# Up-projection of the last two superblocks by Strassen's algorithm, in a transformer block on one Trainium2 core

## The chip, the cores and the metric

One core of one Trainium2 chip runs the whole kernel. Its engines work side by side and wait for each other through semaphores: PE (TensorE, matmuls into PSUM), DVE (VectorE), ACT (ScalarE), POOL (GpSimd), and SP (SyncE), which here issues every DMA. The metric is the device time of one execution in microseconds; the kernel before takes 467.36 us, the median of three runs (466.88 to 467.95).

## The reference

One transformer block over 2048 tokens of 512 features: a modulated layer norm, linear attention with 32 heads and a learned two-sided softmax feature map, a residual; then a second modulated layer norm, and an MLP with 1376 hidden features:

```python
h = _layernorm(x) * (1 + ca) + sa
x = x + ga * A(h)                    # attention: qkv, feature maps, phi_q (phi_k^T V) / den, wo
h = _layernorm(x) * (1 + cb) + sb
y = _layernorm(h)
x = x + gb * (gelu(y @ w1 + b1) @ w2 + b2)
```

The change is in `y @ w1`, the up-projection: (2048 x 512) times (512 x 1376).

## The kernel before, in words

Every large matrix product is made in three matmuls of rounded numbers: an operand is split into a high part (rounded to the fp32r type by ACT) and a low part (what is left, by a subtraction on DVE or POOL), and `mm3` adds high x high, high x low and low x high into one PSUM bank. A matmul contracts 128 features and gives 128 x 512 numbers, so a product with 512 input features takes 4 x 3 = 12 matmuls.

Tokens come in 8 blocks of 256 (b = 0 to 7) for the attention and in 4 superblocks of 512 for the MLP. The first third projects q, k and v and adds up the key-value sums; q is kept in DRAM. Then, for each block: softmax parts and their scaling (tiles eq, ez, rcq; mostly POOL and DVE), transposition through DRAM (eb, et_dram, eT), the product with the sums (po), the output projection (pw), and the second pair of layer norms in three steps, la, lb and lc, each with statistics on DVE and a power on POOL (rsb, rsc). The result h goes through a DVE transposition (yb) to DRAM (yt_dram), comes back as yf, and `y_split` makes its high and low parts, yT.

A superblock's MLP: `up(b, fc)` makes one of 11 chunks of 128 hidden features (the last holds 96) in a bank pg, applies the GELU on ACT and splits the result into g; `down(b, fc)` multiplies g with w2 into four banks py, one for 128 tokens each, that gather over all chunks. `mlp_out` adds py to x and stores it. While superblock b's MLP runs, the attention of blocks 2b+2 and 2b+3 runs beside it; superblock 3 has nothing beside it.

The order of the work is written out by hand. `Later` and `Held` hold back every instruction under the name of its item, the engine's letter (p PE, a ACT, v DVE, g POOL, s SP) and its part of the program; `nc.issue()` then takes them in the order of the strings in `ISSUE`. Each engine runs its instructions in that order, so an instruction that waits holds up all behind it on its engine. `SLOTS` says which of 19 equal SBUF buffers and of 8 PSUM banks a tile takes. Weights of the up-projection lie in SBUF as high and low parts for the whole program (w, wlast), those of the down-projection in w2a and w2b.

Because all instructions are issued by `Later`, every row of the profile carries one line number; instructions are told apart by their tiles.

Of the kernel before, what the change touches and what calls it, by code (L numbers as in the profile page):

```python
# [47 lines left out]
    "e93cf0idhabf4g55a2h17e4i27ce25986gi96f88af4a115357h8gbbf584dec522e4g0bai8761904137ecd23b5bh77df6ae2i"  # L48
    "8507c4i322a9h829i53i9a528962i4bafe6a8h7b52ge1d00gcfggf19dgd0d2c56g9ceecc6eb0c0gc87h0g9f37i53ffb62ci7"
    "c45450fab338f8fb8c78b4374hg7h8d14263afbaab619aae55df204db9bf32fb313dd9bhe3047gagi11e",  # L50
    "bank":
    "1264710140570135353253136162435026621304533162143502472521023727652170445605353123554624602715375317"
    "153573175304761253153253215213576546037217123132712723327513246406462",
    "st6a": "01110010",
    "sta": "01010101",
    "vea": "10101001",
    "rsa": "01110110",
    "nma": "10001001",
    "dz": "001001011",
    "mxk": "1010100110011010",  # L60
    "smk": "0100011001010101",
    "rck": "0010011010101001",
    "mxq": "01011011",
    "smq": "00000000",
    "rcq": "02002110",
    "den": "10000010",
    "rd": "11010110",
    "st6b0": "10111000",
    "stb0": "01010111",
    "veb0": "01100100",  # L70
    "rsb0": "01110010",
    "st6c0": "11010100",
    "stc0": "11001000",
    "vec0": "00110010",
    "rsc0": "11011010",
    "nmc0": "11110010",
    "st6b1": "11110111",
    "stb1": "00000011",
    "veb1": "10111001",
    "rsb1": "01101110",  # L80
    "st6c1": "11100001",
    "stc1": "01000010",
    "vec1": "10100011",
    "rsc1": "01000111",
    "nmc1": "11011001",
# [3 lines left out]
-init.v -init.v -init.p db.s x0.s x1.s dk.s dq.s dm.s si.a si.v dk.s si.v bd.v si.v dk.s sr.p dq.s s0.v s0.v s0.v  # L89
s0.v s0.v s0.v s0.g sr.a dm.s s1.v s1.v s1.v n0.v s1.v n0.v dm.s s1.v s1.v n0.v s1.g fk.p dm.s ok.a x.s fq.p n0.a  # L90
ok.v fq.p oq.a n1.v n1.v m.v m.g n1.a h0.p dk.s oq.v fk.p m.v m.a n1.v ++x.s fk.p oq.a f.v ok.a oq.v fq.p n1.a ok.v
fq.p f.a m.g m.v f.v h0.p m.v pf.p n1.v m.a m.g n1.s oq.a f.v ok.a dv.s m.v m.g f.a n1.s m.a f.v pf.p n1.s m.v m.v
oq.a n1.s m.a f.v dv.s fk.p m.v ok.v f.a bg.s f.v +x.s pf.p oq.v f.v s.v f.a ok.a f.v vs.a oq.v q0.p s.v s.v s.v s.v
ok.v n1.s q1.p bg.s s.v ++s.v s.g +bg.s vs.a vs.v vs.g n.v ++s.v n.a n.v pf.p n.a n.v n.v pv1.p bg.g ++s.v k0.v n.s
h.a q0.a +s.v n.s h.a +s.v n.s q1.a +bg.g +s.v ++s.v n.s ++s.v k0.v f.a pv0.p ++++x.s h.a +bg.v f.g +bg.s h.a +s.v
+s.v k0.v f.a +bg.s +s.v ++s.v +bg.s k1.v +s.g k1.v f.g
""",
    """
pk1.p n.v -k0.v n.a n.v +s.g e.v bg.a bg.g -k0.a +bg.s +++s.v -n.s pk0.p e.v ++x.s e.g bg.a -v1.a bg.g bg.v +n.v
+n.v k1.v bg.g bg.a -k1.v q0.p +n.a -k1.v +bg.g n.a bg.v +n.a n.v +bg.g +n.v pv1.p h.a k1.v h.a e.g +n.v +bg.a n.v  # L100
++++x.s bg.a e.g ++s.v h.a n.s q1.p -k0.v e.g h.a n.s q0.a n.s f.a ++s.v +n.s f.a f.g k1.v n.s +++s.v +n.s pv0.p
q1.a k0.v f.g e.a +bg.v ++s.v -k1.a k1.v +bg.s ++s.v ++s.v -k0.v -bg.a
""",
    """
pk1.p +++s.v --k0.g --v0.a +s.v ++s.v bg.v -n.s n.s -bg.v n.s +s.g -k0.v -v1.a pv0.p --v0.v --k1.v bg.g ++s.v +n.v
--v1.v bg.v +n.a +++s.v bg.a pv1.p --bg.v bg.a +n.v bg.v -k0.v +n.a e.v -k1.a n.s h.a ++s.v --k1.v pk0.p e.g h.a
k1.v f.a ++s.v --k1.g e.v h.a +++s.v +++s.v -k0.v q1.p f.g -k1.v -k0.a h.a --v1.v k0.v -v0.a +++s.v -v0.v --v0.v
k1.v f.a k1.v -m0.p f.g -m1.p +n.v bg.p q0.p +n.v e.g bg.a q1.a k0.v +n.s +h.a +++s.v k1.v +n.s +h.a +++s.g -k1.v
+n.s e.g v1.v
""",  # L110
    """
pk1.p -k0.v -bg.s -q0.a -e.g n.s -k0.v h.a -q1.s f.a --e.v --k1.g -k0.a -bg.s ----init.v --v1.v --e.a pk0.p n.s k1.v
-bg.s f.g --v1.v --k0.v h.a -bg.s -bg.s f.a -bg.s +s.g -k0.v f.g
""",
    """
pk0.p --k0.v -k1.v -bg.s ---k0.v ---v0.v -k0.v ---k0.g n.v -k1.v pk1.p n.a -k1.v --v0.a -k0.v --k1.a --k0.g -k0.v
n.v --v0.v +n.v -k0.v n.a pv1.p --k1.v -k0.a --v1.a --k1.v +n.a k0.v --k1.g h.a k1.v --m0.p h.a --m1.p k0.v h.a
-m0.p h.a -bg.g -pv0.p n.v -k1.a --v0.v n.v f.a -k0.v n.s f.a n.s f.g -bg.a --v1.v -k0.v n.s pv0.p +n.v k1.v v1.a
n.s f.g -v1.v -v0.v +n.a k0.v k1.v -bg.g k1.v -pv1.p -k1.v n.s k0.v -bg.g +n.v k0.a +n.v
""",  # L120
    """
pk1.p -k1.a --k1.v n.s -k0.v n.s --v0.a --k0.g --v1.a n.s ----e.v h.a n.s -bg.a pk0.p ----e.s --k1.g -k1.v h.a h.a
-k0.v f.a n.s k1.v h.a -bg.g -bg.s --m1.p k0.v f.a -m0.p --v0.v -v1.v -m1.p +++lp0.s pv0.p v1.v -k1.v f.g k0.v k1.v
f.g ----e.v k1.v
""",
# [73 lines left out]
out.v d.p out.s out.v out.v out.s out.s  # L199
""",  # L200
]
W2A = 6
AHEAD = 4
NT = 1
BUFS = 19
ALIGN = 64
NE = 2


class Held:  # L210

# [958 lines left out]
```

## Time and profile before

| what | value |
|---|---|
| median of three runs | 467.36 us |
| span of the profiled execution | 466.6 us, 0.8 below the median; the page lists no other time of it |
| PE busy | 458.5 us, 98% |
| DVE busy | 317.1 us, 68% |
| POOL busy | 279.7 us, 60% |
| ACT busy | 234.6 us, 50% |
| DMA | 68.05 MB, 146 GB/s on average |

How to read the rows: in a group of instructions stand engine, operation, out<-in with tile names, shape and count, then busy us and mean ns of one, then the idle time of the engine before them and who ended it. In a chain of waits and a timeline each row starts with its start and its length in us. A stretch of the span shows, after the length, the busy us of PE, PEld (weight loads), DVE, ACT and POOL with their instruction counts, then the granted clock, the DMA share and GB/s. A matmul's own duration overlaps with its neighbours', so its price in a stream is read from the chain.

### The profile page before, as it was taken

Reading aid. Unit: us, or ns where it says so; the run is one execution under the profiler, and the core shown is the slowest. Engines: PE = TensorE matmul, PEld = TensorE weight load, DVE = VectorE, ACT = ScalarE, POOL = GpSimd, SP = SyncE. Lnnn points to the kernel's source line nnn. Section 1 sums busy time; section 2 is a strip of 40 time slices with the busy share of each in tenths; the row PEclk is TensorE's granted clock in tenths of the full one; section 3 lists DMA queues with packets and bytes.
Section 4 is the critical chain, followed back from the end, with each engine's and each line's share of the span. In section 5 each row is a group of like instructions: output and inputs, shape, how many; then the busy total and the mean of one; then the engine's idle time right before and its main releaser. Section 6 shows DMA issues by size and latency. Waiting matters only on the chain.

```text
span 466.6 us, 8536 instructions
## 1 busy us (share of the span) xinstructions
PE 458.5 (98%) x3297; PEld 372.3 (80%) x3297; DVE 317.1 (68%) x612; ACT 234.6 (50%) x381; POOL 279.7 (60%) x233
## 2 busy tenths in 40 slices
PE   8999999999999999999999999999999999999996
PEld 5887888888878878978787878787788788788884
DVE  5999999989938599389797579896484472221113
ACT  4757866767440827848537743176133234422221
POOL 2369587999799998989899684756721020300000
PEclk9999999999999999999999999999999999999999
DMA  8998738492372664836837728077445504000003
GB/s 311 382 311 301 195 84 276 95 269 55 100 257 95 189 209 90 244 104 139 224 135 160 225 53 241 1 130 178 143 90 136 122 14 93 15 30 1 1 1 135
DMA packets 83673, 68.05 MB, mean 146 GB/s; under 512 B 54688, under 2 KB 70960, under 8 KB 83376
## 3 DMA queue, kind: packets, MB, share of 16 engines
q1 hardware_dynamic: 83632, 67.50, 50.9%
q8 instruction: 26, 0.43, 0.4%
q14 instruction: 15, 0.12, 0.1%
HBM read 44.94 MB, written 22.55 MB: 145 GB/s over the span
## 4 chain that ended last, share of the span: by engine, by line
PE 85%; DMA 5%; DVE 4%; POOL 2%; issue 1%; ACT 1%; SPq 0%; DVEq 0%; POOLq 0%; ACTq 0%
PE py L218 25%; PE pg L218 24%; PE pv L218 8%; PE pk L218 8%; PE pw L218 8%; PE pq L218 7%; PE pkv L218 2%; DMA wm<-in_wmodT 2%; PE po L218 1%; DVE pw L218 1%; DMA eT<-et_dram 1%; DMA wms<-in_wmodT 1%; DMA xt<-in_x 1%; PE qp L218 1%; POOL w2a L218 1%
## 5 line engine op out<-in xcount | busy, mean ns | idle before, releaser
L218 PE MATMUL pg<-yT,w 128*128 128x512 f32 (+1 forms) x528 | 115.3, 371 | 0.6 <-DVE yT L218 0.3
L218 PEld LDWEIGHTS pg<-yT,w 128*128 128x128 f32 x528 | 92.8, 188 | 18.5 <-DVE yT L218 0.5
L218 ACT ACTIVATE pg<-pg,blob 128x512 f32<-128x512 f32 x44 | 29.1, 662 | 100.6 <-PE pg L218 100.4
L218 PE MATMUL py<-w2a,g 128*128 128x512 f32 x288 | 70.7, 391 | 0.0
L218 DVE TENSOR_TENSOR g<-pg,g 128x512 fp32r<-128x512 f32 x40 | 27.2, 680 | 61.7 <-ACT g L218 61.7
L218 PEld LDWEIGHTS py<-w2a,g 128*128 128x128 f32 x288 | 53.6, 188 | 12.6 <-issue 1.6
L218 PE MATMUL pk<-wk,hT 128*128 128x512 f32 x192 | 46.2, 392 | 0.8 <-ACT hT L218 0.7
L218 PE MATMUL py<-w2b,g 128*128 128x512 f32 x192 | 46.9, 391 | 0.0
L218 PE MATMUL pv<-wvh,hT 128*128 128x512 f32 x192 | 45.9, 392 | 0.0
L218 PE MATMUL pw<-wo,oT 128*128 128x512 f32 x192 | 45.4, 390 | 0.0
L218 PE MATMUL pq<-wq,hT 128*128 128x512 f32 x192 | 45.3, 391 | 0.0
L218 PEld LDWEIGHTS pk<-wk,hT 128*128 128x128 f32 x192 | 35.6, 188 | 9.1 <-ACT hT L218 1.1
L218 PEld LDWEIGHTS py<-w2b,g 128*128 128x128 f32 x192 | 35.9, 188 | 8.1 <-issue 0.7
L218 PEld LDWEIGHTS pw<-wo,oT 128*128 128x128 f32 x192 | 35.9, 188 | 7.8 <-issue 0.4
L218 PEld LDWEIGHTS pv<-wvh,hT 128*128 128x128 f32 x192 | 35.7, 188 | 7.5
L218 PEld LDWEIGHTS pq<-wq,hT 128*128 128x128 f32 x192 | 35.8, 188 | 7.3
L218 POOL TENSOR_TENSOR ez<-eq,zb 128x1024 f32<-128x1024 f32 x15 | 36.8, 2469 | 5.5 <-ACT last L218 3.0
L218 POOL TENSOR_TENSOR yT<-yf,yT 128x256 fp32r<-128x256 f32 x24 | 17.2, 742 | 35.1 <-ACT yT L218 35.0
L218 POOL TENSOR_TENSOR ek<-ek,rck 128x1024 f32<-128x1024 f32 x16 | 30.8, 1939 | 4.5 <-DVE rck L218 2.3
L218 POOL TENSOR_TENSOR eq<-eq,rcq 128x1024 f32<-128x1024 f32 x15 | 28.9, 1937 | 0.3
L218 ACT ACTIVATE g<-pg 128x512 fp32r<-128x512 f32 x40 | 24.0, 599 | 9.5 <-PE pg L218 4.4
L218 DVE TENSOR_REDUCE smq<-eq 128x64 f32<-128x1024 f32 x16 | 19.2, 1207 | 6.8 <-ACT eq L218 6.8
(153 smaller groups left out, 783.4 us busy)
## 6 DMA issues: line engine op xcount, KB each, us to landing
et_dram<-eb SPq DMA_DIRECT2D x48, 128.0 KB, 2.9
eT<-et_dram SPq DMA_DIRECT2D x12, 512.0 KB, 5.1
xt<-in_x SPq DMA_DIRECT2D x8, 512.0 KB, 6.1
wms<-in_wmodT SPq DMA_DIRECT2D x8, 512.0 KB, 5.9
x<-in_x SPq DMA_DIRECT2D x8, 512.0 KB, 5.2
out<-x SPq DMA_DIRECT2D x15, 256.0 KB, 2.5
nt_dram<-nb SPq DMA_DIRECT2D x28, 128.0 KB, 3.4
hd<-nt_dram SPq DMA_DIRECT2D x7, 512.0 KB, 5.5
```

The source lines that it names most:

```text
L218: return lambda *a, **k: self.later.hold(self.letter, lambda: f(*a, **k))
```

## The change

Superblocks 2 and 3 are no longer two MLPs one after the other. For each of five pairs of hidden chunks (2j, 2j+1), the pair and the two superblocks form a 2 x 2 product: two chunks of weights by two halves of the 512 input features, times two halves of the features by two superblocks. Winograd's form of Strassen's algorithm makes it from seven half products (each 2 x 3 = 6 matmuls) instead of eight:

- `even(j)`: chunk 2j of superblock 2 from two half products as usual; the first of them is also kept (tile s1) for later.
- `weight_sums(j)`: loads the pair's weights again, makes four sums of them on POOL, and puts their high and low parts over the weights that are no longer needed (and into a new tile, sum1).
- `token_sums(h)`: for each half of the tokens, four differences of the two superblocks' inputs on DVE (tiles yr and tz), and their high and low parts (t14, t23).
- `odd(j)`: the other five half products, into banks pb and pc, with additions on DVE into u tiles between them; gives chunk 2j+1 of superblock 2 and both chunks of superblock 3.

The down-projection of superblock 2 is cut in two: its even and last chunks are gathered first and added to x; the odd ones are gathered at the very end, in one bank for each 128 tokens, and added then. The inputs of superblocks 2 and 3 are read as they lie in DRAM, without the rearrangement that `y_split` made; so x of these tokens is written to DRAM (x1_dram) and read back in the same order (x1n), and the host does not rearrange the second half of the output.

All strings of `SLOTS` and `ISSUE` are new; in the first part the opening rows stand nearly as before. There are 20 equal buffers instead of 19; the small statistics tiles mostly have one buffer.

```diff
+    def half_product(o, w, t, first):
+        for k in range(2):
+            for wj, tj in ((0, 0), (0, 1), (1, 0)):
+                nc.tensor.matmul(o, w[wj][:, k], t[tj][:, k], start=first and k + wj + tj == 0, stop=k + wj == 2,
+                                 skip_group_check=True)
 ...
         if b < NY:
             return
         yT = y_half(b)
+        if b >= 4:
+            for k2 in range(2):
+                src = YF[b][:, 2 * k2:2 * k2 + 2]
+                nc.scalar.activation(yT[0][k2], src, AF.Copy)
+                nc.gpsimd.tensor_sub(yT[1][k2], src, f32(yT[0][k2]))
+            return
 ...
+    def even(j):
+        nc.item(f"u{j}")
+        p = ps_mm("pg")
+        (a11, a12), _ = pair(j)
+        half_product(p, a11, [h[0] for h in YT[2]], True)
+        if j % 2 == 0:
+            PS["s"] = wtile("s1", [2, 512])
+        S1[j] = PS["s"][:, j % 2]
+        nc.scalar.activation(S1[j], p, AF.Copy)
+        half_product(p, a12, [h[1] for h in YT[2]], False)
+        G[2, 2 * j] = gelu(p, 2 * j)
+
+    def weight_sums(j):
+        nc.item(f"s{j}")
+        t = wtile("w1s", [KC, 2 * P])
+        nc.sync.dma_start(t, w1[:, :, 2 * j * P:2 * (j + 1) * P])
+        (a11, a12), (a21, a22) = [[t[:, 2 * k:2 * k + 2, m * P:(m + 1) * P] for k in range(2)] for m in range(2)]
+        nc.gpsimd.tensor_add(a22, a21, a22)
+        nc.gpsimd.tensor_sub(a21, a11, a21)
+        nc.gpsimd.tensor_sub(a11, a22, a11)
+        nc.gpsimd.tensor_sub(a12, a12, a11)
 ...
+        for dst, src in ((s3, a21), (sum1, a22), (s24, t[:, :, :P])):
+            nc.scalar.activation(dst[0], src, AF.Copy)
+            nc.gpsimd.tensor_sub(dst[1], src, f32(dst[0]))
 ...
+    def token_sums(h):
 ...
+        for n, dst, p, q, lo in ((1, b11, b12, b11, nc.gpsimd), (2, t2, b22, b11, nc.vector),
+                                 (3, t3, b22, b12, nc.gpsimd), (4, b21, b21, t2, nc.vector)):
+            nc.vector.tensor_sub(dst, p, q)
+            hi, low = [v[:, :, 256 * h:256 * h + 256] for v in TS[n]]
+            nc.scalar.activation(hi, dst, AF.Copy)
+            lo.tensor_sub(low, dst, f32(hi))
+
+    def odd(j):
+        sum1, s2, s3, s4, a22 = SW[j]
 ...
+        p, c = ps_mm("pb"), ps_mm("pc")
+        half_product(p, s2, TS[2], True)
+        nc.vector.tensor_add(u2, p, S1[j])
+        half_product(p, s3, TS[3], False)
+        nc.vector.tensor_add(u3, p, S1[j])
+        half_product(p, a22, TS[4], False)
+        nc.vector.tensor_add(p, p, S1[j])
+        nc.item(f"e{j}")
+        G[2, 2 * j + 1] = gelu(p, 2 * j + 1)
+        nc.item(f"c{j}")
+        half_product(c, sum1, TS[1], True)
+        nc.vector.tensor_add(u3, c, u3)
+        half_product(c, s4, [h[1] for h in YT[3]], False)
+        nc.vector.tensor_add(c, c, u2)
+        nc.item(f"f{j}")
+        G[3, 2 * j + 1] = gelu(u3, 2 * j + 1, nc.gpsimd)
+        nc.item(f"g{j}")
+        G[3, 2 * j] = gelu(c, 2 * j)
 ...
+    for i in range(4):
+        py = ps_acc("py")
 ...
+        for j in range(NJ):
+            down_full(py, 2, 2 * j + 1, i, j == 0, j == NJ - 1)
+        nc.item("out2")
+        add_out(2, i, py, 2 if i == 3 else 1)
```

How the instructions stand. On PE before, where superblock 2 ends and superblock 3 begins (py: down-projection of superblock 2; pg: a chunk of superblock 3 from its inputs yT_846 to yT_849):

```order
L218 MATMUL py_742<-last_370,last_369 128x512
L218 MATMUL py_743<-last_370,last_369 128x512
L218 MATMUL py_740<-wlast,glast 128x512 x2
L218 MATMUL py_741<-wlast,glast 128x512 x2
L218 MATMUL pg<-yT_846,w_376 128x512
L218 MATMUL pg<-yT_848,w_376 128x512
```

On PE now, where superblock 2's even and last chunks have been gathered and the odd products begin (t_856 to t_859 are high and low parts of token sums, t_855 the other two sums, sum_829 a weight sum):

```order
L232 MATMUL py_835<-wlast,glast 128x512 x2
L232 MATMUL py_836<-wlast,glast 128x512 x2
L232 MATMUL pb<-t_856,w_380 128x512
L232 MATMUL pb<-t_857,w_380 128x512
...
L232 MATMUL pb<-t_856,w_380 128x512
L232 MATMUL pc<-t_855,sum_829 128x512 x6
...
L232 MATMUL pb<-t_858,w_380 128x512
L232 MATMUL pb<-t_859,w_380 128x512
```

The matmuls behind superblock 2's gathering read sums of both superblocks, where they read superblock 3 alone; 144 matmuls, all of superblock 2, stand between pw of block 7 and them.

On DVE before, from the last transposition of block 7 on:

```order
L218 STREAM_TRANSPOSE yb<-h_838 128x16x32 x2
L218 TENSOR_TENSOR g<-pg,g 128x512 x2
L218 TENSOR_TENSOR glast<-pg,glast 96x512
L218 TENSOR_TENSOR g<-pg,g 128x512
L218 TENSOR_TENSOR x_645<-py_740,x_645 128x512
L218 TENSOR_TENSOR x_645<-py_741,x_645 128x512
```

and now, the token sums of both halves and the first additions on products:

```order
L232 STREAM_TRANSPOSE yb<-h_820 128x16x32 x2
L232 TENSOR_TENSOR g<-pg,g 128x512 x2
L232 TENSOR_TENSOR yr<-yf,yr 128x512
L232 TENSOR_TENSOR tz<-yf,yr 128x512
L232 TENSOR_TENSOR t_857<-tz,t_856 128x2x256
L232 TENSOR_TENSOR tz<-yf 128x512
L232 TENSOR_TENSOR yr<-yr,tz 128x512
...
L232 TENSOR_TENSOR t_855<-yr,t_855 128x2x256
L232 TENSOR_TENSOR u<-pb,s_831 128x512 x2
```

Twelve rows with both operands in SBUF stand between block 7's transposition and the additions that PE's second half products wait for.

On POOL at the same place, before (the last powers of block 7, then the splits of superblock 3's inputs, and nothing after):

```order
L218 TENSOR_TENSOR rsc_833<-vec_832,mhalf 128x1
L218 TENSOR_TENSOR rsc_837<-vec_836,mhalf 128x1
L218 TENSOR_TENSOR yT_848<-yf,yT_846 128x256
L218 TENSOR_TENSOR yT_849<-yf,yT_847 128x256
L218 TENSOR_TENSOR yT_848<-yf,yT_846 128x256 x2
L218 TENSOR_TENSOR yT_849<-yf,yT_847 128x256 x3
```

and now (w1s: sums of weights; w and sum: their low parts; t: low parts of token sums):

```order
L232 TENSOR_TENSOR rsc_815<-vec_814,mhalf 128x1
L232 TENSOR_TENSOR rsc_819<-vec_818,mhalf 128x1
L232 TENSOR_TENSOR w_380<-w1s,w_380 128x2x128
L232 TENSOR_TENSOR sum_829<-w1s,sum_829 128x256
L232 TENSOR_TENSOR w_380<-w1s,w_380 128x4x128
L232 TENSOR_TENSOR w1s<-w1s 128x2x128
L232 TENSOR_TENSOR t_855<-yr,t_855 128x2x256
L232 TENSOR_TENSOR w_381<-w1s,w_381 128x4x128
L232 TENSOR_TENSOR t_855<-yr,t_855 128x2x256
L232 TENSOR_TENSOR t_859<-tz,t_858 128x2x256 x2
L232 TENSOR_TENSOR yT_827<-yf,yT_825 128x2x256 x2
L232 TENSOR_TENSOR yT_828<-yf,yT_826 128x2x256 x2
```

Five weight splits and sums stand between block 7's last power and the token splits, and the splits of superblock 3's own inputs behind those.

More of the change, by code (lines that the diff above doesn't have):

```diff
@@ new lines, in adaln_hedgehog_mixer @@
+    nc.part += 1
+    for j in range(NJ):
+        weight_sums(j)
+    for h in range(2):
+        token_sums(h)
+    nc.item("ul")
+    up(3, NFC - 1)
+    nc.item("d")
+    down(3, NFC - 1, True, False)
+    for j in range(NJ):
+        odd(j)
+        nc.item("d")
+        for fc in (2 * j + 1, 2 * j):
+            down(3, fc, False, fc == 2 * NJ - 2)
+    nc.part += 1
+    py = PY.pop(3)
+    for q in range(2):
+        x1_natural(6 + q)
+        nc.item("out")
+        for i in range(2 * q, 2 * q + 2):
+            add_out(3, i, py[i])
```

409 lines of the change are left out of this document (239 added, 170 removed).

## The prediction

> **What bounds the kernel now.** First I read the busy times of the page, then the matmul queue's list of waits, then stretches of the span.
>
> ```profile
> PE 458.5 (98%) x3297; PEld 372.3 (80%) x3297; DVE 317.1 (68%) x612; ACT 234.6 (50%) x381; POOL 279.7 (60%) x233
> PEclk9999999999999999999999999999999999999999
> PE warm L218 <- DVE mhalf L218: 0.9, 1, 0.9
> PE fold L218 <- DMA k<-in_wkT: 0.9, 1, 0.9
> PE pk L218 <- ACT hT L218: 0.7, 1, 0.7
> ...
> PE po L218 <- DMA eT<-et_dram: 0.2, 1, 0.2
> PE pk L218 <- POOL hT L218: 0.2, 1, 0.2
> ```
>
> PE is busy in 98% of the span at the full granted clock, and its eight listed waits are under 1 us each; nearly all lie in the opening. So the kernel is bound by the number of matmuls, and no other engine decides its end. "Busy" says nothing on the price of one, since matmuls overlap; that comes from the chain that ended last, which counts them end to end:
>
> ```profile
> 68.48 10.88 PE pk L218 x48
> 330.66 5.46 PE pw L218 x24
> ...
> 366.61 5.44 PE pw L218 x24
> 372.05 2.04 PE py L218 x9
> 394.49 7.00 PE py L218 x31
> ```
>
> 10.88/48 = 0.2267 us for one 128x512 matmul in a stream, and 5.44/24 gives the same. The last superblock starts behind the py row of 394.49, at 401.5, and its last matmul ends at 462.7 (rows of the tail, below).
>
> Stretches of the span (PE, PEld, DVE, ACT, POOL busy us):
>
> ```profile
> 120.00:343.00 223.00, 221.57 (x1539) 179.91 (x1538) 166.66 (x282) 119.46 (x179) 181.62 (x152) 1.00 0.55 151
> 343.00:376.00 33.00, 33.00 (x174) 26.71 (x173) 19.51 (x43) 7.40 (x12) 2.16 (x4) 1.00 0.56 128
> 376.00:402.00 26.00, 26.00 (x117) 21.11 (x116) 9.53 (x19) 11.96 (x25) 7.81 (x12) 1.00 0.19 42
> 402.00:463.00 61.00, 60.70 (x266) 49.27 (x264) 12.43 (x19) 15.56 (x27) 0.00 (x0) 1.00 0.06 23
> ```
>
> From 402 on DVE works 12.4 of 61 us and POOL not at all: the last superblock has matmuls and little else. From 120 to 343 DVE is free for 56.3 us and POOL for 41.4.
>
> **The change, part by part.**
>
> *Matmuls.* For each of five pairs of hidden chunks, superblocks 2 and 3 took 2 x 2 x 12 = 48 matmuls in the up-projection; seven half products of six are 42. That is 30 fewer, all 128x512. All others stay (the down-projection of superblock 2's odd chunks only moves to the end). 30 x 0.2267 = **-6.8 us**, as long as PE never waits longer than now. The Trainium skill, "TensorE: Matmul & The Clock Gate", section "Back-to-back issue gap", gives about 216 ns for an isolated matmul of 512 columns and 131 for sustained streams of loads and matmuls; by the first the saving would be an estimated 6.5 us, by the second 3.9. This trace's 226.7 ns decides, and it is nearer the first.
>
> *Added work beside it,* by rows of the same shape:
>
> ```profile
> L218 DVE TENSOR_TENSOR g<-pg,g 128x512 fp32r<-128x512 f32 x40 | 27.2, 680 | 61.7 <-ACT g L218 61.7
> L218 POOL TENSOR_TENSOR yT<-yf,yT 128x256 fp32r<-128x256 f32 x24 | 17.2, 742 | 35.1 <-ACT yT L218 35.0
> L218 POOL TENSOR_TENSOR hT<-hf,hT 128x512 fp32r<-128x512 f32 x14 | 18.0, 1294 | 2.9 <-ACT hT L218 2.9
> L218 ACT ACTIVATE g<-pg 128x512 fp32r<-128x512 f32 x40 | 24.0, 599 | 9.5 <-PE pg L218 4.4 <-POOL wlast L218 2.7 <-PE pw L218 1.3
> ```
>
> DVE: 25 additions on products, 12 for the token sums, 4 more output additions, 5 splits handed to POOL: net 36 x 0.68 = 24.5 us, to about 342. POOL: weight sums 30 x 0.742 + 5 x 1.294 = 28.7; four token splits and five g splits 9 x 1.294 = 11.6; the yT splits regrouped, -1.5: 38.8 us, to about 319. ACT: 5 copies, 8 token and 15 weight roundings, some 12 us, against six table loads fewer. SP issues 27 more DMAs. All of it would fit under 460 us of matmuls (DVE 74%, POOL 69%), so on average it costs nothing. What can cost is where it must be ready.
>
> *Where the deadline moves.* Count back from the last matmul, 462.7 - 6.8 = 455.9. From the first odd product on, PE has 150 half-product matmuls, 12 for the last chunk of superblock 3, 132 down-projections of it and 60 deferred ones: 354 x 0.2267 = 80.3 us, so it starts at 375.6. Ahead of it stand the even chunks of superblock 2 and their down-projection, 144 matmuls, 32.6 us; so pw of block 7, the last attention block, must be done at 343.0 instead of 372.05: **29 us earlier**. Cover from the later MLP is given up there.
>
> *Can block 7's tail follow in 32.6 us?* In the trace before:
>
> ```profile
> 372.09 0.70 DVE L218 TENSOR_TENSOR pw<-pw,x 128x512 f32<-128x512 f32 x1 [1.31 <-PE pw L218]
> 384.81 1.38 DVE L218 STREAM_TRANSPOSE yb<-h 128x512 f32<-128x512 f32 x2 [0.33 <-ACT h L218]
> 390.74 0.38 SPq L218 DMA_DIRECT2D yf<-yt_dram  x1
> 395.72 0.41 ACT L218 ACTIVATE yT<-yf 128x256 fp32r<-128x256 f32 x1
> 397.23 4.33 POOL L218 TENSOR_TENSOR yT<-yf,yT 128x256 fp32r<-128x256 f32 x6 [10.68 <-ACT yT L218]
> ```
>
> From the end of pw (372.05) to yf landed and in use (395.72): 23.7 us, 9.5 of it from the last transpose (386.2) through two DMAs. Behind that the change needs two DVE subtractions, a rounding and a split for each half of the tokens before the first odd product: some 4 us. 27.7 of 32.6: 4.9 us to spare for block 7 alone. But pw of block 6 now ends only 10.4 us of matmuls before that of block 7 (the chain's pw rows: 336.1 and 372.05), so DVE carries both tails. By its order, 60 DVE rows from block 6's first addition to block 7's transposes add up to 32 us of durations, some 28 us elapsed, as successive rows overlap by an eighth (the 0.70 us row above starts its successor 0.61 later). From block 6's first pw half to the first odd product are 47.4 us of matmuls: 47.4 - 28 - 9.5 - 4 = 5.9 us to spare. Bounds on PE's wait here: 0, if the rows run as densely as that; and upward by POOL's locks, below. I take 0.3 us.
>
> *POOL against DVE.* The trace shows them excluding each other:
>
> ```profile
> 141.07 1.22 DVE L218 TENSOR_REDUCE dz<-ez 128x64 f32<-128x1024 f32 x1 [2.74 <-POOL ez L218]
> 143.32 1.09 POOL L218 TENSOR_TENSOR eq<-mxq,pq 128x512 f32<-128x512 f32 x1
> 143.33 2.16 DVE L218 TENSOR_TENSOR ez<-eq,zb 128x1024 f32<-128x1024 f32 x1
> 144.35 3.41 POOL L218 TENSOR_TENSOR ez<-eq,zb 128x1024 f32<-128x1024 f32 x1
> ```
>
> DVE's ez, with two operands in SBUF, ends 1.08 us behind the POOL row that started 0.01 earlier, and POOL's next ez ends 2.27 behind DVE's: each waited out the other. The reduction of 141.07, one SBUF operand, kept its 1.22 under a running POOL row. So I count as blocked the 12 token-sum rows, which have both operands in SBUF, and none of those with a PSUM operand. Each of the 12 can lose about one POOL row of that stretch, 1.29: **15.5 us** together as the upper bound, 0 as the lower; three of them stand in line behind block 7's landing, 3.9 us, which is inside the 5.9. The Trainium skill, "SBUF — State Buffer", section "Who interferes with whom", states it as a rule: a DVE instruction with two SBUF inputs and a GpSimd instruction that reads SBUF take one port in turn, each for its whole length. The four rows agree.
>
> *The attention exponentials earlier.* POOL must scale eq of block 7 some 20 us before po of that block (block 2: scaled at 179.8, po at 200). By the same count back from the end (122.6 us of matmuls), po of block 7 is at 333 now, so the scaling by 313, where it was 340.3:
>
> ```profile
> 336.43 3.83 POOL L218 TENSOR_TENSOR eq<-eq,rcq 128x1024 f32<-128x1024 f32 x2
> 177.85 1.94 POOL L218 TENSOR_TENSOR eq<-eq,rcq 128x1024 f32<-128x1024 f32 x1
> 193.29 6.65 DMA eT<-et_dram
> ```
>
> POOL's rows up to there add up to 9 us less than before, so it must find 18 of its 41.4 idle us. That is possible, since it mostly waited for DVE, which had 56 free; if it found half, PE would wait 9 us. I take 0.2.
>
> *Opening.* Four fold products (1.05 us) that filled a wait for hT now stand behind the pk matmuls, and DVE reaches hp of that step 0.76 us sooner:
>
> ```profile
> 17.63 1.65 PE L218 MATMUL pk<-wk,hT 128*128 128x512 f32 x6 [0.68 <-ACT hT L218]
> 19.12 1.05 PE L218 MATMUL fold<-bd,k 128*128 128x128 f32 x8
> ```
>
> Between -0.7 (that wait gone) and +1.1 us; I take +0.2, as the two nearly cancel.
>
> *Tail.* The last output is again two halves of an addition and a DMA: 0.
>
> ```profile
> 462.07 0.63 PE L218 MATMUL py<-wlast,glast 128*128 128x512 f32 x2
> 462.74 0.76 DVE L218 TENSOR_TENSOR x<-py,x 128x256 f32<-128x256 f32 x2 [0.48 <-PE py L218]
> ```
>
> *Sum* on the profiled execution: 466.6 - 6.8 + 0.3 + 0.2 + 0.2 = 460.5 us of span. The page gives no time but the span; the median of the runs is 0.76 above it. Forecast **461.3 us**.
>
> **The rivals.**
>
> *The gain is partly lost at one of the two deadlines.* Block 6's or 7's eT, or the token sums, come 2 to 5 us late: 463.3 to 466.3. For it: PE had slack at neither place to spare (9 to 18 us must be found on POOL). Against it: the free time is there, and in the trace before PE lost 0.2 us in all to eT.
>
> *Token sums late, slower.* The 12 DVE rows and POOL's weight splits, which stand in the same stretch, wait each other out, DVE's lateness delays ACT's roundings, and these POOL's splits. At the full 15.5 us, less the 5.9 spare, PE would wait 9.6 us at the first odd products: 461.3 + 9.3 = 470.6. It turns into a loss once the stretch is late by more than 5.9 + 6.8 = 12.7 us. Against it: the path holds three of the twelve; the deadlines of the other sums come 1.4 to 9 us later.
>
> *The odd products wait on their own additions.* Each pair reads P6, P6+P7 and so on out of the same bank between half products; if PE waited there 0.68 us and a hand-over for each of 15 additions, some 10 us would go and about nothing or a loss be left. Against it: PE's order has two to four other half products (1.4 us each) between most dependent ones.
>
> **How the numbers follow.** Forecast with waits up to 2 us: 0.60, range 459.8 to 463.0. Partly lost: 0.21. Token sums late: 0.10; the odd products' own waits: 0.09. Faster means below 466.4 (0.2% under the median, about what a measurement of this kernel can tell from no change): the first two, 0.81. Of the other two, 0.06 ends within 0.2%, where the waits just eat the gain, and 0.13 above. The range: low 459.6, the sum with no added wait (460.6) less the opening's 0.7 and a little for the runs' spread; high 467.0, which takes in the partly lost gain.
>
> **What would show it.** 30 matmul rows fewer, each 0.227 us in the chain; PE's wait for eT and at the first pb under 1 us each; DVE near 342 and POOL near 319 us busy; the last DVE row about 3.5 us before the end. Wrong would be: waits of PE for t, sum or w over 2 us, DVE's yr, tz or t rows far over 0.7 us and ahead of a late pb, or a gain from fewer waits than now.

## The result, and the profile after

| | before | after |
|---|---|---|
| median of the timed runs | 467.60 us (4 runs, 466.88 to 467.95) | 463.67 us (4 runs, 462.58 to 464.27) |
| ratio | | 0.9906, 95% interval 0.9884 to 0.9928 |
| span of the profiled execution | 466.6 us | 461.9 us |
| forecast | | 461.3 us, range 459.6 to 467.0 |

The kernel became faster by 3.9 us. The forecast had the direction and the mechanism, and stood 2.4 us too low: of a gain of 6.1 us, some two thirds came. The time lies inside the stated range, but above the 459.8 to 463.0 us of its main case; it fell where the rival "partly lost" stood. Where the rest of the gain is, is the question of the experiments.

The busy line of the page of the changed kernel:

```profile
PE 453.9 (98%) x3267; PEld 365.5 (79%) x3267; DVE 345.2 (75%) x648; ACT 239.4 (52%) x395; POOL 318.6 (69%) x269
```

30 matmul rows fewer, DVE at 345.2 (342 forecast) and POOL at 318.6 (319). PE's list of waits, changed kernel:

```profile
PE warm L232 <- DVE mhalf L232: 0.9, 1, 0.9
PE pw L232 <- ACT h L232: 0.7, 1, 0.7
PE zp L232 <- ACT kvT L232: 0.5, 1, 0.5
PE pk L232 <- ACT hT L232: 0.5, 1, 0.5
PE pkv L232 <- POOL ek L232: 0.4, 1, 0.4
PE pg L232 <- POOL yT L232: 0.3, 1, 0.3
PE pc L232 <- DVE ek L232: 0.3, 1, 0.3
PE fold L232 <- DMA k<-in_wkT: 0.2, 1, 0.2
```

No wait for t, sum or w, the three that were to show the forecast wrong; but pw, pkv and pc, three that were not among the eight of before (po and a second pk have gone). This pc is a single small product at 73 us, not the bank of the odd products. The chain that ended last, changed kernel, in two pieces:

```profile
317.37 2.72 PE pw L232 x12
320.09 1.02 PE po L232 x32
321.11 2.94 PE py L232 x12
...
331.86 3.01 PE pw L232 x12
...
339.97 5.45 PE pw L232 x24
...
378.19 2.72 PE pb L232 x12
```

The odd stage went as forecast: the first odd product comes 32.8 us behind the end of block 7's pw (345.42; 32.6 forecast) and its twelve matmuls take 2.72 us, 0.2267 each. From that pw to the end, 498 matmuls start within 112.80 us, 0.2265 each, so the rival by which the odd products wait for their own additions did not come about. But pw of block 7 ends 2.4 us later than the 343.0 of the forecast, so what is missing inside the span was lost ahead of it. The same rows show a second price. Twelve matmuls that run on take 2.72 us (317.37); twelve behind a change of stream (321.11) take 2.94. Behind a wait (331.86) the row of 3.01 counts from the first start to the last end, which is 2.88 for twelve that run on (378.03, below), so it is 0.13 longer, beside the wait. From the start times of all PE records, such a restart costs 0.09 us at the change and 0.11 at the second matmul behind a change or a wait. From 40 us on, 46 matmuls of the trace before start 0.30 to 0.36 us behind the one ahead, and 56 of the trace after: 1.0 us.

Stretches of 20 us (PE busy, count, granted clock), before:

```profile
120.00:140.00 20.00, 19.45 (x393) 1.00 0.53 184
180.00:200.00 20.00, 19.12 (x149) 1.00 0.66 172
240.00:260.00 20.00, 20.00 (x91) 1.00 0.68 159
320.00:340.00 20.00, 20.00 (x117) 1.00 0.49 135
```

and after:

```profile
120.00:140.00 20.00, 19.04 (x449) 1.00 0.63 225
180.00:200.00 20.00, 20.00 (x138) 1.00 0.76 214
240.00:260.00 20.00, 19.55 (x87) 1.00 0.80 192
320.00:340.00 20.00, 19.26 (x138) 1.00 0.90 249
```

PE idled 1.43 us in these four before and 2.15 after; with 40 to 120 us (80.00 busy of 80 before, 79.71 after) and 260 to 280 (20.00 and 19.92) that is 1.1 us more. Idle time and restarts together are some 2.1 us, and with 6.8 us of matmuls they make the 4.7 us by which the profiled span fell (the opening, the tail and small differences cancel).

A second count, by start times, agrees. The zp products (the sum over all keys) start at 135.66 us before and at 134.00 after, where 12 pq matmuls, 2.7 us, stand behind them instead of ahead: 1.1 us are lost ahead of zp. From zp to the end of the last matmul PE takes 327.04 us before and 324.23 after; with the 12 matmuls more and the 30 fewer it would be 322.96, so 1.3 us are lost behind zp. The tail gives 0.2 back.

### The profile page after: what moved, and what is told of

Same layout as the page of the kernel before. It is cut to its first block, busy times and chain, and to the rows that moved or that the text cites. A ratio compares the mean times of both kernels' runs of the same rounds, so it can differ in the third digit from the quotient of the medians.

```text
span 461.9 us, 8663 instructions
## 1 busy us (share of the span) xinstructions
PE 453.9 (98%) x3267; PEld 365.5 (79%) x3267; DVE 345.2 (75%) x648; ACT 239.4 (52%) x395; POOL 318.6 (69%) x269
## 4 chain that ended last, share of the span: by engine, by line
PE 83%; DMA 5%; DVE 3%; POOL 3%; ACT 3%; SPq 2%; issue 1%; DVEq 0%; ACTq 0%; POOLq 0%
PE py L232 24%; PE pg L232 14%; PE pw L232 9%; PE pq L232 8%; PE pk L232 8%; PE pv L232 7%; PE pb L232 4%; PE pc L232 3%; PE po L232 2%; PE pkv L232 2%; SPq L232 2%; DMA eT<-et_dram 2%; DMA wm<-in_wmodT 2%; POOL x L232 1%; DMA x<-in_x 1%
## 5 line engine op out<-in xcount | busy, mean ns | idle before, releaser
L232 PE MATMUL pg<-yT,w 128*128 128x512 f32 (+1 forms) x348 | 72.0, 362 | 0.5 <-POOL yT L232 0.3
L232 PE MATMUL py<-w2a,g 128*128 128x512 f32 x288 | 69.0, 391 | 0.0
L232 PEld LDWEIGHTS pg<-yT,w 128*128 128x128 f32 x348 | 58.5, 189 | 12.0 <-POOL yT L232 1.1
L232 ACT ACTIVATE pg<-pg,blob 128x512 f32<-128x512 f32 x29 | 19.2, 660 | 33.5 <-PE pg L232 33.3
L232 POOL TENSOR_TENSOR eq<-eq,rcq 128x1024 f32<-128x1024 f32 x15 | 30.0, 2006 | 0.4
L232 POOL TENSOR_TENSOR g<-u,g 128x512 fp32r<-128x512 f32 x5 | 6.4, 1288 | 32.7 <-ACT g L232 32.7
L232 DVE TENSOR_REDUCE dz<-ez 128x64 f32<-128x1024 f32 x16 | 18.9, 1199 | 9.7 <-POOL ez L232 9.6
L232 POOL TENSOR_TENSOR w<-w1s,w 128x1024 fp32r<-128x1024 f32 (+2 forms) x15 | 22.5, 1502 | 1.3 <-issue 1.2
L232 ACT ACTIVATE ek<-ek 128x1024 f32<-128x1024 f32 x16 | 16.9, 1056 | 10.8 <-DVE ek L232 9.1
```

What stands on the lines that cost most here:

```text
L232: return lambda *a, **k: self.later.hold(self.letter, lambda: f(*a, **k))
```

## The experiments

The kernel before ran beside every group of runs; each ratio is to its runs of that group. The groups ran on different chips, so between groups the ratios count, not the times. "Stream" is PE's time from the start of the zp products (the sum over all keys, at 134) to the end of the last matmul, in the profiled execution; it leaves out the opening, where the span of one kernel varies by 1 to 2 us.

| kernel | time, us | ratio, 95% interval | stream, us |
|---|---|---|---|
| before, unchanged | 468.19 | 1.0008 (0.9996 to 1.0019) | |
| before, small DMA scratch | 468.96 | 1.0010 (0.9995 to 1.0025) | |
| changed, 30 matmuls put back | 471.20 | 1.0066 (1.0047 to 1.0084) | 331.2 |
| changed, h rows first | 463.91 | 0.9907 (0.9880 to 0.9935) | 323.4 |
| changed, unchanged | 463.92 | 0.9914 (0.9900 to 0.9928) | 324.0 |
| changed, h rows and keys first | 463.82 | 0.9911 (0.9897 to 0.9925) | 323.7 |
| changed, token sums 6 rows late | 467.97 | 1.0003 (0.9985 to 1.0021) | 328.2 |
| changed, two splits to DVE | 464.18 | 0.9918 (0.9896 to 0.9941) | 324.1 |
| h rows, keys, other buffers | 463.24 | 0.9889 (0.9871 to 0.9906) | 324.3 |
| the same, stores later | 465.34 | 0.9941 (0.9924 to 0.9958) | 325.2 |
| the same, x load later | 463.23 | 0.9890 (0.9869 to 0.9910) | 323.1 |
| changed, no weight sums | 464.02 | 0.9906 (0.9885 to 0.9926) | 323.7 |

(In the changed kernel's first profile the stream is 324.2.)

**What lies outside the span.** The kernel before as it is, and with one argument of the change:

```
-    nc = bacc.Bacc("TRN2", ..., num_devices=1)
+    nc = bacc.Bacc("TRN2", ..., num_devices=1, dynamic_dma_scratch_size=1024)
```

> The kernel before, unchanged, so that its spans stand beside its times. The prediction set its median time 0.76 us above its span (467.36 against 466.6). The changed kernel's four runs lie 1.74 to 1.81 us above theirs. Theory A, something outside the span grew with the change: time minus span here is 0.4 to 1.3 us, and about 1 us of the gain that is missing (463.7 measured, 461.3 forecast) lies outside the span. Rival B, the profiled span of before was simply of a longer execution and the part outside is 1.8 us in both: the spans here are near 465.8, and nothing is lost outside; then the span's own gain is only 3.9 us.

> The kernel before with one argument of the change alone: the 1024-byte DMA scratch. If this argument is what lengthens the part outside the span, time minus span is 1.8 us and the ratio to before about 1.002 (1 us longer). If it is not, span and time stay as in the unchanged kernel, ratio 1.000. A change of the span itself (over 0.5 us) would speak for moved addresses on the chip's memory, which no theory here asks for.

Rival B holds. In all 131 executions of this study whose span is on record, time minus span is 1.73 to 1.85 us; the scratch argument changes neither. The profiled execution of before, 466.6 us of span, therefore took 468.4, and was 0.8 us longer than the median of its kernel; the prediction subtracted the 466.6 from a median that belongs to another execution and found 0.76. 1.0 us of the error is this step.

**The price of 30 matmuls.** Put back by running one of seven half products twice:

```
         half_product(c, sum1, TS[1], True)
+        half_product(c, sum1, TS[1], True)
```

> The changed kernel with 30 matmuls put back: in each of the five odd steps the half product of the weight sum and the first token sum runs twice (the second run starts its bank anew, so the numbers stay). It is the prediction's first term by itself. Theory, 0.2267 us each and all in the last stretch, where PE waits for nothing: span +6.8, so 468.7 to 468.8, slower than before. Rival, sustained matmuls as cheap as 131 ns: +3.9. Rival, the odd stage waits on its additions and the repeats fill holes: clearly less than 6.8.

PE's zp and last rows, 30 matmuls put back:

```profile
134.05 1.99 PE L232 MATMUL zp<-kvT,blob 128*128 128x256 f32 x8 [0.55 <-ACT kvT L232]
463.73 1.52 PE L232 MATMUL py<-w2b,g 128*128 128x512 f32 x6
```

and of the changed kernel:

```profile
134.00 1.99 PE L232 MATMUL zp<-kvT,blob 128*128 128x256 f32 x8 [0.55 <-ACT kvT L232]
456.70 1.52 PE L232 MATMUL py<-w2b,g 128*128 128x512 f32 x6
```

The last group starts 7.03 us later, and with 0.05 of it at zp the stream is 6.98 us longer; the median is 7.3 us longer than the 463.91 of the variant of the changed kernel in the same group (h rows first, below). The 468.7 to 468.8 of the expectation is a span, and the span of this profile is 468.9. So the prediction's first term is right, 6.8 to 7.0 us, and no hole in the odd stage would have hidden a part. The Trainium skill, "TensorE: Matmul & The Clock Gate", section "Back-to-back issue gap", would have given 3.9 us by its sustained 131 ns; this run disagrees with it, at 233 ns each.

**How much time block 7's line has to spare.** Six more DVE rows in the path from block 7's landing to the first odd product:

```
-            nc.vector.tensor_sub(dst, p, q)
+            if (h, n) == (1, 1):
+                nc.hold("v", lambda dst=dst, p=p, q=q: [tc.nc.vector.tensor_sub(dst, p, q) for _ in range(7)])
+            else:
+                nc.vector.tensor_sub(dst, p, q)
```

> The changed kernel with the first of the last half's token sums computed seven times over (each time with its sign turned, so the seventh is the first): six DVE rows of two SBUF operands, 6 x 0.69 = 4.1 us, in the line from block 7's landing to the first odd product. The prediction gave this line 5.9 us to spare. By the prediction, nothing happens: PE's wait at the first pb stays under 0.5 us and the span within 0.5 us of the changed kernel. By the trace of after, in which the line ends 0.05 us ahead of the product, all of it shows: PE waits 4 us or more at the first pb and the time is 467.7 or more; with POOL's rows locking the six out in turn, up to 7 us.

The line in the changed kernel (yf is the landed half, yr and tz the sums, t their rounded parts):

```profile
373.35 0.69 DVE L232 TENSOR_TENSOR yr<-yf,yr 128x512 f32<-128x512 f32 x1 [0.62 <-DMA yf<-yt_dram]
374.14 0.69 DVE L232 TENSOR_TENSOR tz<-yf,yr 128x512 f32<-128x512 f32 x1
375.44 0.61 ACT L232 ACTIVATE t<-yr 128x512 fp32r<-128x512 f32 x1
376.13 1.30 POOL L232 TENSOR_TENSOR t<-yr,t 128x512 fp32r<-128x512 f32 x1 [4.55 <-ACT t L232]
376.61 1.37 DVE L232 TENSOR_TENSOR t<-tz,t 128x512 fp32r<-128x512 f32 x1 [1.77 <-ACT t L232]
378.03 2.88 PE L232 MATMUL pb<-t,w 128*128 128x512 f32 x12
```

and with six rows more:

```profile
373.87 5.05 DVE L1208 TENSOR_TENSOR yr<-yf,yr 128x512 f32<-128x512 f32 x7 [0.57 <-DMA yf<-yt_dram]
378.96 0.63 ACT L232 ACTIVATE t<-yr 128x512 fp32r<-128x512 f32 x1 [2.84 <-DVE yr L1208]
380.42 1.07 DVE L232 TENSOR_TENSOR t<-tz,t 128x512 fp32r<-128x512 f32 x1 [0.70 <-ACT t L232]
380.44 0.50 PE L232 MATMUL pb<-t,w 128*128 128x512 f32 x1 [1.68 <-ACT t L232]
381.54 4.39 PE L232 MATMUL pb<-t,w 128*128 128x512 f32 x11 [0.60 <-DVE t L232]
```

and the stretch behind these waits (PE, PEld, DVE, ACT, POOL busy us, then the granted clock):

```profile
380.40:386.00 5.60, 4.96 (x14) 3.69 (x15) 2.31 (x4) 1.72 (x4) 3.65 (x4) 0.70 0.00 0
```

The seven rows take 5.05 us instead of 0.69: 4.36 us late. PE started its first two pb matmuls 2.75 us behind the stream in all (by start times, the pw of block 7 as origin), so 1.6 us were absorbed, not 5.9. They are there because ACT reached t<-yr in the changed kernel 1.4 us after its input (374.04 to 375.44, it had other rows in its queue), and because the last t row ends a little ahead of the matmul that reads it. That is the second matmul of the product, as the waits of the late run show (the first waits for ACT's t, the second for DVE's): it starts at 378.25, so the row that ends at 377.98 has 0.27 us, not the 0.05 to the product's start. The expectation by the trace of after failed too: PE lost 2.75 us here and not 4 or more, and its time of 467.7 or more came true only by what follows.

The loss was larger than PE's wait: time +4.05 us, and 4.5 us in the profile between pw of block 7 and the end. The stretch shows why: the granted clock is 0.70 over its 5.6 us (0.50 from 382.2 to 385.7 and 1.00 around it), and seven of the next twelve matmuls come 0.427 us behind the one before instead of 0.227. The Trainium skill, "TensorE: Matmul & The Clock Gate", Part 1, has 426.7 ns for 512 columns on a cold clock, with which the trace agrees, and lets the clock fall after an idle window of about 3.4 us; here it fell after 1.8 and 0.9 us of lost time with one matmul between. It does not fall in every execution: of the eight of this kernel, five show a mean granted clock of 0.993 to 0.996 and take 467.73 to 470.53 us, three show 0.999 or 1.000 and take 466.70, 466.81 and 467.79. A single wait of 2.0 us (stores later, below) left the clock at 1.00 in the profiled execution; one of the six executions of that kernel, its longest, has a mean of 0.996, so a fall there cannot be ruled out.

**Is it POOL that delays the token sums?** Two of the second half's splits moved from POOL to DVE, the busier engine:

```
+            if h == 1 and lo is nc.gpsimd:
+                nc.name, lo = "t1x", nc.vector
             lo.tensor_sub(low, dst, f32(hi))
+            nc.name = f"t{h}"
```

(The name puts the two rows into DVE's order where they stood in POOL's.)

> The changed kernel with two splits of the last half's token sums moved from POOL to DVE, which has more to do: 2 x 0.68 us more on DVE, 2 x 1.29 less on POOL. If POOL's row (376.13 to 377.43) locks DVE's t row (376.61, it takes 1.37 where the shape takes 0.69), the line to the first odd product ends 0.3 to 0.6 us sooner in spite of the added row, and DVE's t rows take 0.69. If it was something else, each added row delays it by 0.68 and PE waits 0.6 us at the first pb. The time moves by less than 0.5 us in the first case, since PE does not wait there.

```profile
374.11 0.69 DVE L232 TENSOR_TENSOR yr<-yf,yr 128x512 f32<-128x512 f32 x1 [0.83 <-DMA yf<-yt_dram]
376.66 0.69 DVE L232 TENSOR_TENSOR t<-yr,t 128x512 fp32r<-128x512 f32 x1 [1.06 <-ACT t L232]
377.27 0.69 DVE L232 TENSOR_TENSOR t<-tz,t 128x512 fp32r<-128x512 f32 x1
378.56 2.88 PE L232 MATMUL pb<-t,w 128*128 128x512 f32 x12
```

With one row more to do, DVE ends the line 0.60 us ahead of the product (377.96 to 378.56) instead of 0.05 (377.98 to 378.03), and both its rows take 0.69. So POOL's row of 376.13 was the delay. In the changed kernel the t row of 376.61 ends 0.55 us behind that POOL row (377.98 and 377.43), and the one of 369.40 (below) as far behind POOL's split of 368.59. The Trainium skill, "SBUF — State Buffer", section "Who interferes with whom", gives the rule that the prediction quotes, one of the two waiting out the other; the run agrees. The time does not fall, as expected, since PE did not wait there.

**Does the work on the weights cost anything?** The weight sums left out whole (loads, sums, roundings, splits; the odd products read the plain weights):

> The changed kernel without its weight sums: the five loads, the 20 sums on POOL, the 15 roundings on ACT and the 15 splits on POOL are left out, and the odd products run on the weights as they are, so the output is not the reference's. PE's, DVE's and all other work stays. The prediction put this work at nothing, because POOL and ACT have time for it. If that holds, the time stays at 463.7 to 464.0. If it crowds the stretch of 290 to 345 (ACT's queue ahead of the h row, transfers against the eT and yf loads), PE's waits there go: 0.3 to 1.0 us less. If it is what makes the line to the first odd product just in time (POOL's rows against DVE's), DVE's token-sum rows all take 0.69 us and the line ends 1 us or more sooner; PE does not wait there, so the time shows nothing of that.

```profile
PE 454.5 (98%) x3267; PEld 365.3 (79%) x3267; DVE 343.8 (74%) x648; ACT 233.7 (51%) x380; POOL 290.8 (63%) x234
```

27.8 us of POOL and 5.7 of ACT less, and the time is 464.02, ratio 0.9906: no change that these runs can tell. The trace shows a small one: the stream is 323.7 us, 0.4 to 0.6 shorter than in the two profiles of the changed kernel, and 0.25 of that lies between pw of block 7 and the first odd product. The line to the first odd product then ends 1.4 us ahead of it (376.82 to 378.20), so the sums do lie on that line's shoulders. Not all of DVE's token-sum rows went to 0.69, as was expected: three still take 1.01, 1.16 and 1.48, beside splits on POOL that remain. "Hidden" is right for this work to about half a us, and the larger part of the missing gain is not in it.

**PE's new waits, one by one.** First ACT's order ahead of 331:

```
-yf0.a ... +++s2.a ... +++s2.a ... u.a u.a lc10.a u.a ... lc11.a u.a u.a
+yf0.a ...                         u.a u.a lc10.a lc11.a u.a ... u.a u.a +++s2.a +++s2.a
```

> The changed kernel with ACT's order altered in one place: block 5's two h rows (which free the bank that block 6's pw matmuls wait for at 331) go ahead of two roundings of weight sums and the rounding of the last chunk's rows, about 1.9 us earlier. Theory, PE's largest wait (0.9 us at 331.86) comes from ACT's queue, into which the weight sums were put: that wait is gone and the time falls by 0.9 to 1.0 us, to 462.7. Rival, the token sums are just in time: they end 0.05 us ahead of the first odd product in the changed kernel (DVE's t row 376.61 to 377.98, the product at 378.03), so what is won at 331 comes back as a wait at the first pb, and the time stays within 0.3 us. Between the two, if the token sums follow pw of block 7 forward, the first holds.

In the changed kernel ACT's rows stand in one line without a gap, and PE waits for the last:

```profile
328.43 1.20 ACT L232 ACTIVATE glast<-pg 128x512 fp32r<-128x512 f32 x2
329.65 0.78 ACT L232 ACTIVATE h<-pw,nmc,rsc 128x512 f32<-128x512 f32 x1
330.45 0.55 ACT L232 ACTIVATE last<-pg 32x128 fp32r<-32x128 f32 x2
331.03 0.78 ACT L232 ACTIVATE h<-pw,nmc,rsc 128x512 f32<-128x512 f32 x1
331.86 2.33 PE L232 MATMUL pw<-wo,oT 128*128 128x512 f32 x9 [0.74 <-ACT h L232]
```

With h first that wait is gone, nothing comes back at the first pb, and the stream is 323.4, 0.8 us shorter; the time did not show it (463.91, where 462.7 was expected; this profile lost 1.1 us in the opening, at 30.8, where pv waited for its weights). Then the unchanged kernel again, and the keys first at 127 as well:

> The changed kernel again, unchanged, beside its variants on one chip. Part of the span outside PE's stream is settled (time minus span was 1.73 to 1.84 us in every run of every kernel so far), so the forecast of 461.3 was 1.0 us too low for that alone and should have read 462.3. Expected: the same waits as in its first profile (331: 0.9 us, 132: 0.5, 256: 0.3 and 0.6), time 463.7 to 464.0, ratio 0.990 to 0.991. If the waits are chance, another set of them shows up here.

> The changed kernel with two of PE's new waits taken away by order alone: the h rows ahead of the weight sums' roundings on ACT, as in the run before, and at 127 the key scaling of the last two blocks ahead of a query row on POOL, with their reciprocals ahead of the query sums on DVE. Theory, the missing gain is made of such waits in the middle of the program: 0.8 us (331, as the trace of the h rows' run showed between the z products and the end) and 0.5 us (132) less than the unchanged changed kernel of this call, 462.4 to 462.6, ratio 0.987 to 0.988. Rival, the query rows that go back cost as much at the z products or the first token's chain: only 0.8. Rival, the token sums or the loads in the opening decide, and waits that go there come back: no difference.

The unchanged kernel's second profile has the same stream within 0.2 us, but its wait at 331 was 0.25 us instead of 0.9. PE came to the place 0.6 us later, mostly because it had lost more at 257 to 271; ACT ended the h row at 331.8 in both. So that wait was a meeting time, and its price depends on what PE lost before. The weight sums alone did not make it: in the run without them it is 0.25 us as well (ACT's h row 331.42 to 332.20, the pw matmul at 332.25). What is left there is the rounding of the last chunk's rows ahead of h. And the second order failed by a buffer:

```profile
129.51 0.55 DVE L232 RECIPROCAL rck<-smk 128x64 f32<-128x64 f32 x1 [2.00 <-POOL ek L232]
134.68 1.26 PE L232 MATMUL pkv<-ek,vf 128*17 128x32 f32 x128 [0.83 <-POOL ek L232]
```

DVE's reciprocal writes the small buffer that POOL's key row still read, so it stood 2.0 us, and the keys came later than before instead of sooner. The order of that run, and the buffers of the two last keys swapped in the next:

```
-a0.g: eq<-mxq,pq   k1.g: ek   k0.g: ek                     (POOL, from 127)
+k1.g: ek   k0.g: ek   a0.g: eq<-mxq,pq
-e.v: rcq   e.v: smq   k1.v: rck   k0.v: smk   k0.v: rck    (DVE, from 125)
+k1.v: rck   e.v: rcq   k0.v: smk   k0.v: rck   e.v: smq
-    "rck": "0111101010110010",                             (next run only)
+    "rck": "0111101010110001",
```

> The two changes of order of the run before once more, with one buffer choice beside them: in that run DVE's reciprocal at 129.5 waited 2.0 us for POOL's key row, because both use the same one of two small buffers; here the last two swap their buffers. Theory, PE's extra waits in the middle can be taken away one by one: pkv's wait at 132 (0.5) and pw's at 331 (0.25 to 0.9) are gone, PE's stream from the z products to its end is 0.3 to 0.9 us shorter than the 324.0 to 324.2 us of the two profiles of the changed kernel, and the time 0.7 to 1.0 us lower: 462.9 to 463.2, ratio 0.988 to 0.990. Rival, such waits come back further on: 463.7 to 464.0 as in the run before.

Both waits are gone (pkv and pw are not in its list of waits), and the median is 463.24. pkv's lies ahead of zp, so the stream does not show it, and the stream is 324.3 all the same, since at 266 the eT load took 7.9 us and po waited 0.7: in this trace the rival held. Two attempts at that one:

```
 eT<-et_dram x2        eT<-et_dram x2
 x<-in_x          ->   x<-in_x
 out<-x x2             w1s<-in_w                 (stores later)
 w1s<-in_w             out<-x x2
```

> The kernel of the run beside it, with two stores of superblock 0's rows issued behind the next load of weights (about 5 us later). In the changed kernel the last eT load of block 4 takes 7.3 us to land (258.7 to 266.0), with 1 MB of an x load and two stores issued right behind it, and PE's po waits 0.25 to 0.5 us for it. Theory, the transfers behind it slow it: it lands in 4 to 5 us and that wait goes, 0.3 us less than the run beside it. Rival, the x load alone does it, or the stores then slow the load that follows: no difference.

```profile
270.10 0.60 ACT L232 ACTIVATE oT<-po 128x512 fp32r<-128x512 f32 x1 [3.85 <-DMA out<-x]
272.08 3.02 PE L232 MATMUL pw<-wo,oT 128*128 128x512 f32 x12 [1.87 <-DVE g L232]
```

po's wait is gone (eT landed in 5.5 us), and a worse one has come: ACT's oT row writes the buffer that the stores read, so a later store is a later pw. (The wait of pw names DVE's g, which stands in DVE's order behind an oT row of its own, and that one waited 3.0 us for ACT's.) In the other attempt the x load moves behind the weights' load, and the stores stay:

> The kernel with the two reorderings and the swapped buffers, in which block 4's x load goes behind the next load of weights on SP (264 instead of 259), while the two stores stay where they are. In the run that moved the stores the eT wait (0.87 us in the kernel beside it) went, but the wait of pw grew to 2.0 us: ACT's oT row writes the buffer that these stores read, and it began when they had landed (270.0 and 270.1). Theory: what is issued right behind the eT load slows it and the stores alike; without the x load eT lands at 264 to 265 and the stores at 266 to 267 instead of 268 to 269, so both waits go, x is still there 4 us ahead of its use at 274, and PE's stream from the z products to the end falls from 324.3 to 323.2 to 323.6 us; time 0.5 to 0.9 us under the kernel with the reorderings, 462.4 to 462.8. Rival: the stores alone slow eT as much, or x now comes late at 274: no gain, 463.2 or more.

```profile
266.36 0.60 ACT L232 ACTIVATE oT<-po 128x512 fp32r<-128x512 f32 x1 [0.41 <-PE po L232]
```

eT now lands in 5.3 us and the stores by 264.6 instead of 269.0, neither po nor pw waits, and the stream is 323.1, the shortest of all; 1.1 of the 1.3 us lost behind zp are back. The theory of this run holds in the trace. The median, 463.23, does not fall below that of the order without the later x load: five runs from 462.02 to 463.82 do not tell 0.5 us, and the profiled execution is the fastest of the five. The kernels with other buffers and with the later x load have medians 0.4 to 0.7 us under the changed kernel's, and ratios whose intervals reach just into its own, so they are probably a little faster, and no more can be said.

## Why the prediction was right, and where it was wrong

**Matmuls, -6.8:** right. Put back, they cost 7.0 us in the trace and 7.3 in the medians.

**Added work hidden:** right to about half a us. DVE came out 3.2 us above the forecast of its busy time and POOL 0.4 below; all of the weight work left out changes no median, and the stream by 0.4 to 0.6 us.

**The deadline's place:** right, 32.8 us against 32.6. **Its spare time, 5.9 us:** wrong; 1.6. Block 7 took 27.9 us from the end of pw (345.42) to yf in use (373.35), where the trace before had 23.7. Measured, the DVE part up to the first store (345.42 to 364.53) took 19.1 us against 14.1 before, the DMAs 8.8 against 9.5, and the sums 4.6 against 4. The step that failed is the 28 us for DVE's rows of both blocks:

```profile
330.50:364.50 34.00, 33.26 (x173) 25.74 (x172) 28.49 (x60) 19.55 (x38) 22.23 (x29) 1.00 0.83 228
363.79 0.71 DVE L232 STREAM_TRANSPOSE yb<-h 128x512 f32<-128x512 f32 x1 [1.16 <-ACT h L232]
```

The 60 rows are there and keep DVE busy for 28.5 us, the 28 of the forecast; but from the end of block 6's first pw half (330.5) to the last transposition (364.5) 34.0 us pass. DVE stood still for 5.5 of them, mostly for rows of ACT, whose queue the prediction did not count on this line. The last of these pauses is shown; ahead of that h row ACT's queue holds roundings of weight sums. And 4.9 us, the prediction's own sum for block 7 alone, was less than the 5.9 that it went on with. The term "+0.3" came true, as 0, by luck: the line was just in time. The rival "token sums late, slower" was nearer than its 0.10: it begins to cost at 1.6 us of lateness, not at 5.9, and 4.4 us eat the whole gain, since in most executions the clock falls too (467.97, ratio 1.0003), not the 12.7 that the prediction gave.

**POOL against DVE:** right in kind and near the lower bound. Of the twelve rows, four are longer than 0.69 us in the changed kernel, 3.0 us together of at most 15.5 (three here, the fourth is the 376.61 above). Ten of the twelve stand ahead of the first additions, two behind them. The moved splits show the cause for the row of 376.61, and the run without weight sums for that of 370.35, which takes 0.68 us where POOL's split of a weight sum (369.84 to 371.58) is gone; for the other two it is read from the times:

```profile
369.40 1.03 DVE L232 TENSOR_TENSOR t<-tz,t 128x512 fp32r<-128x512 f32 x1 [0.76 <-ACT t L232]
370.35 1.77 DVE L232 TENSOR_TENSOR tz<-yf 128x512 f32<-128x512 f32 x1
...
382.15 1.56 DVE L232 TENSOR_TENSOR yr<-yr,tz 128x512 f32<-128x512 f32 x1
```

**eT:** POOL scaled eq of block 7 in time (306.8 to 311.4, 313 needed), and po of block 7 did not wait. The 0.2 us fell elsewhere: po of block 4, 0.2 to 0.9 us by run, by start times.

**Opening +0.2:** 0.1, by the first pq (21.39 before, 21.51 after); second profiles of the two kernels have 20.94 and 20.66, so nothing can be told. **Tail 0:** -0.2 (3.9 and 3.7 us behind the last matmul).

**The sum** failed in two terms. Added waits were put at 0.7 us, all at places that the change's own data reach; the rest of the program, whose order on every engine had also been changed, was put at 0, and in all 2.1 us were lost, 1.1 in idle time and about 1.0 in restarts. PE idled 1.6 us more at 120 to 140, 240 to 260 and 320 to 340, 0.4 more at two other places, and 0.9 less at 180 to 200. One reading made the middle look safe: "nearly all" of the eight listed waits of before were said to lie in the opening, but four of them, 1.4 us together, lie between 135 and 200 us. This is the rival "gain partly lost" in size, with a mechanism that it did not name. And the part outside the span was taken as 0.76 us where it is 1.8. Of 2.4 us of error, 1.4 are the first and 1.0 the second.

What stays open: which single wait ends up costing what, since they trade with each other from run to run. Behind zp the order alone took back 1.1 of the 1.3 us in one trace (a stream of 323.1 against 324.2, where 322.96 would be as good as the kernel before); medians and ratios put it at 0.4 to 1.2 us, with intervals as wide. The 1.1 us ahead of zp were attacked at pkv alone, and the two waits at 257 (0.3 to 0.5 and 0.6 us by start times) not at all.

## What to carry to other kernels

When a change comes with a new order, price the order too: count the places at which the bound engine changes its stream and give each a few tenths, even where the old profile lists no wait. Work out a new deadline's slack from the whole queue of every engine on the line, the pauses in which one waits for another too, and then ask what one microsecond of lateness does, as here a slack of 1.6 us carried a gain of 4. And take the constant between span and time from executions of which both are known, never from a median and another execution's span.

## What was not expected of the hardware

- A change of PE's stream costs about 0.2 us (2.94 us for twelve matmuls instead of 2.72), even where no wait is listed, and a wait about 0.1 us more than its length (3.01 instead of 2.88 from first start to last end).
- Lost time of 2.75 us, in two pieces, let the granted clock fall (0.50 for 3.4 us) and cost 1.7 us more, in five of eight executions; a single loss of 2.0 us did not in the profiled execution.
- A load of 512 KB took 7.2 to 7.9 us to land with 1 MB issued right behind it, and 5.3 to 5.5 with half of that. The amount is not all: at the same place of the kernel before it landed in 4.96 with 768 KB behind it.
